# Attention over a cached sequence, one query: the value product with 8 positions x 64 columns per multiplication instead of 2 positions x 192 columns

## The chip, the core and the metric

The kernel runs on one core of a Trainium2 chip. The core has a matrix engine (TensorE; PE in the profile, with PEld for its weight loads), a vector engine (VectorE, DVE), an activation engine (ScalarE, ACT), a general engine (GpSimd, POOL) and a synchronising engine (SyncE, SP). Here SP issues nearly all transfers from HBM into the on-chip memory; 16 DMA engines carry them out. PE writes its sums into a separate accumulation memory (PSUM), from which DVE and ACT read.

The metric is the device time of one execution in microseconds (us), the median of several runs. The profile comes from one more execution, which has a time of its own.

## The reference

One token goes through a transformer block whose normalisations are modulated by a condition `c`. Nearly all of the data is the cache: 32 heads of 8192 positions of 192 numbers, once for keys and once for values, 32-bit, 201 MB each. Cut to its core:

```python
mod = (silu(c) @ w_mod).reshape(1, 6, 1, 640)
sa, ca, ga, sb, cb, gb = (mod[:, k] for k in range(6))

h = layernorm(x) * (1 + ca) + sa
q = (h @ wq).reshape(1, 1, 32, 192).transpose(0, 2, 1, 3)
scores = einsum("bhqd,bhkd->bhqk", q, k_cache) * 192 ** -0.5
o = einsum("bhqk,bhkd->bhqd", softmax(scores), v_cache)
x = x + ga * (o.transpose(0, 2, 1, 3).reshape(1, 1, 6144) @ wo)

h = layernorm(x) * (1 + cb) + sb
x = x + gb * (relu(h @ w1 + b1) ** 2 @ w2 + b2)
```

## The kernel before

**Layout.** A head's 8192 positions lie on the 128 partitions, 64 consecutive positions on each, so a head's keys are one tile of 128 x 12288 numbers (6.3 MB), and its values another. Three such slots (`slot`, L48) hold keys, values and, at the start and the end, the dense weights. `load` (L149) issues one transfer for a tile; the last heads' tiles are cut in two or four (`CUTS`, L32). All of these transfers are issued by SP in the order of the program: k, the pair's weights, v, head after head. A transfer into a slot waits until the work that read the slot's last tile is done: a k transfer waits for the value multiplications of an earlier head, a v transfer for the key sums of an earlier head.

**Keys** (`keys`, L182). With one query there is no matrix product worth PE's while: in four chunks of 16 positions DVE multiplies the tile by the query, which stands on all partitions (L189), POOL folds six of the sixteen products in half (L192), DVE sums nine (L193) and the six folded ones (L194), and ACT sums one (L197). Between the chunks come pieces of other heads' work, in an order written out by hand (`between`, L272): in even heads `project` of the pair before after chunk 1 and `attend` after chunk 2, in odd heads the next pair's `query` after chunk 2. After chunk 0 comes `inverse` of the head before.

**Softmax** (`softmax`, L211). DVE takes the largest score of each partition, PE spreads these over the partitions with the identity, and DVE takes the largest of all. ACT then writes the exponentials, each 16 times (`p`, 128 x 64 x 16, L221), and their sum per partition, which PE adds over the partitions (`total`, L86). `inverse` (L205) takes one over that sum on DVE and multiplies it by a mask of two columns, which chooses between two positions.

**Values** (`values`, L225). For each of 32 pairs of positions, PE takes the pair's 2 x 16 copies of exponentials as stationary operand (32 columns) and the two positions' 384 numbers as the moving one (L232). The pair's number modulo 4 names the strip of 32 columns of the array, and so the 32 partitions of the sum, to which it is added. The first 16 rows of a strip's sum hold what is wanted in columns 0 to 191, the other 16 in columns 192 to 383; the rest is a product of one position's weight with the other's values.

**Output projection** (`project`, L237, and `attend`, L249). For each head of a pair DVE scales the first half of the sum by the mask's first column (L243), and adds the second half times the second column (L244). Three PE multiplications with ones add the rows and turn the 384 results onto partitions (L247), DVE copies them (L251), and 12 multiplications with the rows of `wo` add to the accumulator `att` (L255).

**The end.** After the last head come the last pair's `project` and `attend`, the second normalisation (its sums over partitions are multiplications with ones, L89), the remaining columns of the modulation (`mod`, L128), and the dense part (L317, L320 to L323, L333). Its weights go into slots as these come free: `w1_t` behind the last keys, `gw_t` behind the last values, the latter in three pieces (L294). The last product (L333) needs the second and third pieces for its second half and its last block.

Of the kernel before, what the change touches and what calls it, by code (L numbers as in the profile page):

```python
# [8 lines left out]
F32 = mybir.dt.float32  # L9
AF = mybir.ActivationFunctionType  # L10
ALU = mybir.AluOpType
AX = mybir.AxisListType

P = 128
D = 640
H = 32
SK = 8192
DH = 192
FF = 1536
G = 4  # L20
DG = D // G
FG = FF // G
KB = DG // 32
FB = FG // 32
PW = 2 * DH
NPAIR = H // 2
NPOS = SK // P
I = 16
# [4 lines left out]
WO = 3 * D  # L33
WQ = KB * PW
W2_CUT = ((0, 6), (6, 5), (11, 1))
# [4 lines left out]
def block_kernel(ctx: ExitStack, tc: tile.TileContext, xc, kc, vc, wq0, wx, wo15, wm0, wm1, w1, gw2, bb, out):  # L40
    nc = tc.nc
    const = ctx.enter_context(tc.tile_pool(name="const", bufs=1))
    strm = ctx.enter_context(tc.tile_pool(name="strm", bufs=3))
    work = ctx.enter_context(tc.tile_pool(name="work", bufs=2))
# [3 lines left out]
    def slot(name):  # L48
        return strm.tile([P, NPOS * DH], F32, tag="slot", name=name, bufs=3)


    ident = const.tile([P, P], F32, name="ident")
    make_identity(nc, ident)
    ones = const.tile([P, P], F32, name="ones")
    nc.vector.memset(ones, 1.0)

    mask = const.tile([P, 2], F32, name="mask")
    nc.vector.memset(mask[:, 0:1], 0.0)
    nc.vector.memset(mask[:, 1:2], 1.0)
    for g in range(G):  # L60
        nc.vector.memset(mask[32 * g:32 * g + 16, 0:1], 1.0)
        nc.vector.memset(mask[32 * g:32 * g + 16, 1:2], 0.0)
    eps_t = const.tile([P, 1], F32, name="eps_t")
    nc.vector.memset(eps_t, EPS)

# [6 lines left out]
    def columns(src, n, name, pool=const, **how):  # L72

        t = pool.tile([P, n // 32, 32], F32, name=name, **how)
        nc.vector.transpose(t.rearrange("p b r -> p (b r)"), src)
        return t
# [9 lines left out]
    def total(src, name):  # L86

        ps = psum.tile([P, 512], F32, tag="sm", name="ps_" + name, bufs=2)
        nc.tensor.matmul(ps[:, :1], ones, src, start=True, stop=True)  # L89
        return ps[:, :1]  # L90
# [23 lines left out]
    e = const.tile([P, KB], F32, name="silu")  # L114
# [22 lines left out]
    def load_w(i):  # L137

        w_t[i] = strm.tile([P, WO + WQ], F32, tag="w", name=f"w{i}", bufs=2)
        if i < 0:  # L140
            nc.sync.dma_start(w_t[i][:, WO:], wq0)
        elif i + 1 == NPAIR:
            nc.sync.dma_start(w_t[i][:, :WO], wo15)
# [3 lines left out]
    k_t, v_t = {}, {}  # L147

    def load(src, to, h, what):  # L149
        to[h] = slot(f"{what}{h}")  # L150
        n = CUTS.get((what, h), 1)
        w = NPOS * DH // n
        for c in range(n):
            nc.sync.dma_start(to[h][:, c * w:(c + 1) * w],
                              src[h].rearrange("(p i) d -> p (i d)", p=P)[:, c * w:(c + 1) * w])

    load_w(-1)
    load(kc, k_t, 0, "k")
# [12 lines left out]
    def query(i):  # L171
        w = w_t[i - 1][:, WO:].rearrange("p (b n) -> p b n", b=KB)
        ps = psum.tile([P, 512], F32, tag="q", name=f"ps_q{i}", bufs=2)
        for b in range(KB):
            nc.tensor.matmul(ps[:, :PW], hR[:, b], w[:, b], start=(b == 0), stop=(b == KB - 1))  # L175
        qb_t[i] = work.tile([P, PW], F32, name=f"qb{i}", tag="qb")
        nc.scalar.activation(qb_t[i], ps[:, :PW], AF.Copy, scale=DH ** -0.5)

# [24 lines left out]
    ri_t, ps_t, sum_t = {}, {}, {}  # L203

    def inverse(h):  # L205
        r = work.tile([P, 1], F32, tag="r", name=f"r{h}")
        nc.vector.reciprocal(r, sum_t.pop(h))
        ri_t[h] = work.tile([P, 2], F32, tag="ri", name=f"ri{h}", bufs=3)
        nc.vector.tensor_scalar(ri_t[h], mask, r, None, op0=ALU.mult)

    def softmax(h, sc):  # L211
        mp = work.tile([P, 1], F32, tag="mp", name=f"mp{h}")
        nc.vector.tensor_reduce(mp, sc, axis=AX.X, op=ALU.max)  # L213
        ps = psum.tile([P, 512], F32, tag="sm", name=f"ps_mx{h}", bufs=2)
        nc.tensor.matmul(ps[:, :P], mp.to_broadcast([P, P]), ident, start=True, stop=True)  # L215
        nm = work.tile([P, 1], F32, tag="nm", name=f"nm{h}")
        nc.vector.tensor_reduce(nm, ps[:, :P], axis=AX.X, op=ALU.max, negate=True)  # L217

        p = work.tile([P, NPOS, 16], F32, tag="p", name=f"p{h}", bufs=1)
        sp = work.tile([P, 1], F32, tag="sp", name=f"sp{h}")  # L220
        nc.scalar.activation(p, sc[:, :, None].to_broadcast([P, NPOS, 16]), AF.Exp, bias=nm, accum_out=sp)  # L221
        sum_t[h] = total(sp, f"sum{h}")
        return p

    def values(h, p):  # L225

        t = v_t.pop(h)
        ps_t[h] = psum.tile([P, 512], F32, tag="o", name=f"ps_o{h}", bufs=3)
        n = NPOS // 2
        for j in range(n):  # L230
            g = j % G
            nc.tensor.matmul(ps_t[h][32 * g:32 * (g + 1), :PW], p[:, 2 * j:2 * j + 2].rearrange("p e r -> p (e r)"),  # L232
                             t[:, PW * j:PW * (j + 1)], start=(j < G), stop=(j >= n - G))

    os_t = {}

    def project(i):  # L237

        os_ = work.tile([P, PW], F32, tag="os", name=f"os{i}")
        for a in range(2):  # L240
            h = 2 * i + a
            o, ps, ri = os_[:, DH * a:DH * (a + 1)], ps_t.pop(h), ri_t.pop(h)
            nc.vector.tensor_scalar(o, ps[:, :DH], ri[:, 0:1], None, op0=ALU.mult)  # L243
            nc.vector.scalar_tensor_tensor(o, ps[:, DH:PW], ri[:, 1:2], o, op0=ALU.mult, op1=ALU.add)  # L244
        os_t[i] = psum.tile([P, 512], F32, tag="sm", name=f"ps_oT{i}", bufs=2)
        for j in range(3):
            nc.tensor.matmul(os_t[i][:, 32 * j:32 * (j + 1)], os_[:, P * j:P * (j + 1)], ones[:, :32], start=True, stop=True)  # L247

    def attend(i):  # L249
        oT = work.tile([P, 96], F32, tag="oT", name=f"oT{i}")  # L250
        nc.vector.tensor_copy(oT, os_t.pop(i)[:, :96])  # L251
        w = w_t.pop(i)[:, :WO].rearrange("p (j n) -> p j n", j=3)
        for j in range(3):
            for g in range(G):
                nc.tensor.matmul(att[32 * g:32 * (g + 1), :DG], oT[:, 32 * j:32 * (j + 1)],  # L255
                                 w[:, j, DG * g:DG * (g + 1)],
                                 start=(i == 0 and j == 0), stop=(i == NPAIR - 1 and j == 2))

    x_t = spread(x_c, KB, "x_t")
    bbt = spread(bbc, FB + KB, "bbt")  # L260
    for h in range(H):
        i = h // 2
# [9 lines left out]
        def between(c):  # L272
            if c == 1 and h % 2 == 0 and h:
                project(i - 1)
            elif c == 2 and h % 2 == 0 and h:
                attend(i - 1)
            elif c == 2 and h % 2 and i + 1 < NPAIR:
                query(i + 1)

        sc = keys(h, between)  # L280
        p = softmax(h, sc)
# [9 lines left out]
    a = 0  # L291
    for b0, n in W2_CUT:
        b = KB * D + (b0 + n) * D
        nc.sync.dma_start(gw_t[:, a:b], gw2[:, a:b])  # L294
        a = b
    w1_t = w1_t[:, :KB * FF].rearrange("p (b n) -> p b n", b=KB)
    w2_t = gw_t[:, KB * D:(KB + FB) * D].rearrange("p (b n) -> p b n", b=FB)

    inverse(H - 1)
    project(NPAIR - 1)  # L300
    attend(NPAIR - 1)
    x1 = const.tile([P, DG], F32, name="x1")
# [12 lines left out]
    for b in range(KB):  # L315
        for g in range(G):
            nc.tensor.matmul(pf[32 * g:32 * (g + 1), :FG], hT2[:, b], w1_t[:, b, FG * g:FG * (g + 1)],  # L317
                             start=(b == 0), stop=(b == KB - 1))
    f = work.tile([P, FG], F32, name="f", tag="spread", bufs=1)
    nc.vector.tensor_add(f, pf[:, :FG], bbt[:, :FG])  # L320
    nc.vector.tensor_scalar(f, f, 0.0, None, op0=ALU.max)
    nc.vector.tensor_mul(f, f, f)
    fT = columns(f, FG, "fT", work, tag="os")  # L323

    mod(5, 1, gw_t[:, :KB * D].rearrange("p (b n) -> p b n", b=KB))
    gb2 = const.tile([P, DG], F32, name="gb2")
# [4 lines left out]
    for b in range(FB):  # L331
        for g in range(G):
            nc.tensor.matmul(py[32 * g:32 * (g + 1), :DG], fT[:, b], w2_t[:, b, DG * g:DG * (g + 1)],  # L333
                             start=(b == 0), stop=(b == FB - 1))
# [45 lines left out]
```

## Time and profile before

| | |
|---|---|
| time, median of 3 runs | 1060.53 us (1060.53 to 1060.59) |
| the profiled execution: time | 1060.67 us |
| the profiled execution: span from the first instruction to the last | 1058.8 us |
| read from HBM | 451.82 MB, 427 GB/s over the span |
| busy: DVE, PE, POOL, ACT | 821.6, 417.6, 180.4, 110.1 us |
| mean granted clock of PE | 0.645 of full speed |

In the profile, a row of a group names the line, the engine, the operation, what it writes and reads (out<-in), the shape and the count; then the busy time in us and the mean duration of one in ns; then the idle time of the engine just before them and what ended most of it. A row of the timeline begins with the start and the duration in us, and the bracket at its end is the idle time before it. A row of the chain of waits has a start, a duration and what set the end in that time. PE's 32-bit multiplications leave two records each, and each record has a weight load.

### The profile page before, as it was taken

Reading aid. Unit: us, or ns where it says so; the run is one execution under the profiler, and the core shown is the slowest. Engines: PE = TensorE matmul, PEld = TensorE weight load, DVE = VectorE, ACT = ScalarE, POOL = GpSimd, SP = SyncE. Lnnn points to the kernel's source line nnn. Section 1 sums busy time; section 2 is a strip of 40 time slices with the busy share of each in tenths; the row PEclk is TensorE's granted clock in tenths of the full one; section 3 lists DMA queues with packets and bytes.
Section 4 is the critical chain, followed back from the end, with each engine's and each line's share of the span. In section 5 each row is a group of like instructions: output and inputs, shape, how many; then the busy total and the mean of one; then the engine's idle time right before and its main releaser. Section 6 shows DMA issues by size and latency. Waiting matters only on the chain.

```text
span 1058.8 us, 7905 instructions
## 1 busy us (share of the span) xinstructions
PE 417.6 (39%) x3120; PEld 188.3 (18%) x3120; DVE 821.6 (78%) x646; ACT 110.1 (10%) x343; POOL 180.4 (17%) x134
## 2 busy tenths in 40 slices
PE   3043532435344144533434353143534424353446
PEld 1011211112121111211111121111212111121223
DVE  2986868878686996868788686897868698689952
ACT  1010101101001010110101010110101101011110
POOL 0211212212111221211212111221212121122210
PEclk8566665666656566665666666566665666666667
DMA  9999999999999999999999999999999999999997
GB/s 399 444 428 420 433 441 419 445 427 430 439 435 418 434 437 436 430 425 430 439 427 433 433 430 435 423 436 440 430 430 431 431 432 435 429 431 430 410 433 300
DMA packets 14013, 452.33 MB, mean 427 GB/s; under 512 B 1812, under 2 KB 1816, under 8 KB 2200
## 3 DMA queue, kind: packets, MB, share of 16 engines
q1 hardware_dynamic: 13688, 451.81, 99.2%
q8 instruction: 24, 0.39, 0.2%
q14 instruction: 13, 0.11, 0.0%
q10 hardware_dynamic: 288, 0.01, 0.0%
HBM read 451.82 MB, written 0.00 MB: 427 GB/s over the span
## 4 chain that ended last, share of the span: by engine, by line
DVE 42%; DMA 40%; PE 15%; ACT 2%; issue 1%; POOL 0%; DVEq 0%; SPq 0%; ACTq 0%
DMA k<-in_kc 36%; DVE k L189 21%; DVE sc L193 12%; PE ps_o L232 11%; DVE sc L194 4%; DMA gw_t<-in_gw 2%; ACT p L221 2%; PE ps_mx L215 1%; DVE os L244 1%; DMA xct<-in_xc 1%; DVE os L243 1%; PE ps_sum L89 1%; PE ps_mod L128 1%; PE ps_q L175 1%; DVE nm L217 0%
## 5 line engine op out<-in xcount | busy, mean ns | idle before, releaser
L189 DVE TENSOR_TENSOR k<-k,qb 128x3072 f32<-128x3072 f32 x128 | 429.0, 3352 | 151.2 <-DMA k<-in_kc 146.8
L192 POOL TENSOR_TENSOR k<-k 128x576 f32<-128x576 f32 x128 | 179.7, 1404 | 835.8 <-DVE k L189 821.1
L193 DVE TENSOR_REDUCE sc<-k 128x9 f32<-128x1728 f32 x128 | 250.2, 1954 | 4.4
L232 PE MATMUL ps_o<-v,p 128*32 128x384 f32 x2048 | 238.9, 636 | 0.0
L215 PE MATMUL ps_mx<-ident,mp 128*128 128x128 f32 x64 | 25.4, 501 | 308.5 <-DVE mp L213 308.5
L197 ACT ACTIVATE jk<-k 128x192 f32<-128x192 f32 x128 | 46.5, 363 | 769.2 <-DVE k L189 751.2
L232 PEld LDWEIGHTS ps_o<-v,p 128*32 128x32 f32 x2048 | 75.5, 139 | 141.9 <-issue 141.3
L247 PE MATMUL ps_oT<-ones,os 128*128 128x32 f32 x96 | 26.5, 400 | 175.9 <-DVE os L244 173.7
L194 DVE TENSOR_REDUCE sc<-k 128x6 f32<-128x576 f32 x128 | 95.0, 743 | 0.1
L215 PEld LDWEIGHTS ps_mx<-ident,mp 128*128 128x128 f32 x64 | 16.0, 311 | 327.4 <-DVE mp L213 302.1
L255 PE MATMUL att<-w,oT 128*32 128x160 f32 x384 | 28.4, 463 | 75.6 <-DVE oT L251 75.6
L247 PEld LDWEIGHTS ps_oT<-ones,os 128*128 128x128 f32 x96 | 22.2, 310 | 189.1 <-DVE os L244 188.5
L175 PE MATMUL ps_q<-w,hR 128*128 128x384 f32 x150 | 52.4, 496 | 0.0
L221 ACT ACTIVATE p<-sc,nm 128x1024 f32<-128x1024 f32 x32 | 36.7, 1147 | 114.2 <-DVE nm L217 114.2
L89 PE MATMUL ps_sum<-sp,ones 128*128 128x1 f32 x64 | 18.8, 363 | 56.2 <-ACT p L221 56.2
L175 PEld LDWEIGHTS ps_q<-w,hR 128*128 128x128 f32 x150 | 27.3, 190 | 25.3 <-issue 9.4
L217 DVE TENSOR_REDUCE nm<-ps_mx 128x1 f32<-128x128 f32 x32 | 9.3, 291 | 28.5 <-PE ps_mx L215 28.5
L255 PEld LDWEIGHTS att<-w,oT 128*32 128x32 f32 x384 | 15.5, 161 | 81.9 <-DVE oT L251 77.7
L89 PEld LDWEIGHTS ps_sum<-sp,ones 128*128 128x128 f32 x64 | 16.1, 312 | 65.6 <-ACT p L221 65.6
L197 ACT ACTIVATION_READ_ACCUMULATOR jk<-k 128x1 f32 x128 | 23.9, 187 | 0.0
L128 PE MATMUL ps_mod<-wm_t,silu 128*32 128x320 f32 (+1 forms) x120 | 12.6, 599 | 12.4 <-DVE silu L118 12.4
L243 DVE TENSOR_SCALAR os<-ps_o,ri 128x192 f32<-128x192 f32 x32 | 13.1, 408 | 5.3 <-PE ps_o L232 5.3
(72 smaller groups left out, 105.5 us busy)
## 6 DMA issues: line engine op xcount, KB each, us to landing
v<-in_vc SPq DMA_DIRECT2D x31, 6144.0 KB, 23.9
k<-in_kc SPq DMA_DIRECT2D x30, 6144.0 KB, 26.8
w<-in_wx SPq DMA_DIRECT2D x15, 1920.0 KB, 32.3
wm_t<-in_wm SPq DMA_DIRECT2D x2, 3200.0 KB, 26.9
k<-in_kc SPq DMA_DIRECT2D x2, 3072.0 KB, 21.8
k<-in_kc SPq DMA_DIRECT2D x4, 1536.0 KB, 21.5
v<-in_vc SPq DMA_DIRECT2D x4, 1536.0 KB, 16.3
w_t<-in_w SPq DMA_DIRECT2D x1, 3840.0 KB, 23.2
```

The costliest lines, as they stand in the source:

```text
L89: nc.tensor.matmul(ps[:, :1], ones, src, start=True, stop=True)
L175: nc.tensor.matmul(ps[:, :PW], hR[:, b], w[:, b], start=(b == 0), stop=(b == KB - 1))
L189: nc.vector.tensor_mul(pr, pr, q[:, None, :].to_broadcast([P, I, DH]))
L192: nc.gpsimd.tensor_add(half, half, pr[:, m:n, DH // 2:])
L193: nc.vector.tensor_reduce(sc[:, c * I:c * I + m], pr[:, :m], axis=AX.X, op=ALU.add)
L194: nc.vector.tensor_reduce(sc[:, c * I + m:c * I + n], half, axis=AX.X, op=ALU.add)
L197: nc.scalar.activation(jk, pr[:, i], AF.Copy, accum_out=sc[:, c * I + i:c * I + i + 1])
L215: nc.tensor.matmul(ps[:, :P], mp.to_broadcast([P, P]), ident, start=True, stop=True)
L221: nc.scalar.activation(p, sc[:, :, None].to_broadcast([P, NPOS, 16]), AF.Exp, bias=nm, accum_out=sp)
L232: nc.tensor.matmul(ps_t[h][32 * g:32 * (g + 1), :PW], p[:, 2 * j:2 * j + 2].rearrange("p e r -> p (e r)"), t[:, PW * j:PW * (j + 1)], star ...
L247: nc.tensor.matmul(os_t[i][:, 32 * j:32 * (j + 1)], os_[:, P * j:P * (j + 1)], ones[:, :32], start=True, stop=True)
L255: nc.tensor.matmul(att[32 * g:32 * (g + 1), :DG], oT[:, 32 * j:32 * (j + 1)], w[:, j, DG * g:DG * (g + 1)], start=(i == 0 and j == 0), sto ...
```

## The change

The value product is laid out otherwise. One multiplication now takes eight positions, four copies of each exponential (again 32 stationary columns), and of each of the eight positions the same 64 of the 192 columns (512 moving columns). A head needs 8 groups of positions times 3 groups of columns (`NV`), 24 multiplications; the column group names the strip, so strips 0 to 2 are used and strip 3 is not. The values are put into this order before the launch. In a strip's sum, row r belongs to position r // 4, and of its 8 blocks of 64 columns only the block of that position is wanted: `project` multiplies the sum by one over the total and by a mask of eight columns in one instruction, and a second one adds the eight blocks. The head's result then stands as 64 columns on 96 partitions, and one multiplication with `quad` (ones in three diagonal blocks of 32 x 32) adds the rows of each strip and turns both heads' results onto partitions. The rows of `wo` are put into the matching order. `inverse` is left with the reciprocal. `kc` is handed over in another shape with the same bytes.

```diff
+E = 8
+ED = 64
+NV = DH // ED
...
-    mask = const.tile([P, 2], F32, name="mask")
-    nc.vector.memset(mask[:, 0:1], 0.0)
-    nc.vector.memset(mask[:, 1:2], 1.0)
-    for g in range(G):
-        nc.vector.memset(mask[32 * g:32 * g + 16, 0:1], 1.0)
-        nc.vector.memset(mask[32 * g:32 * g + 16, 1:2], 0.0)
+    mask = const.tile([P, E], F32, name="mask")
+    nc.vector.tensor_reduce(mask, ident.rearrange("p (g e c) -> p e g c", g=G, e=E), axis=AX.XY, op=ALU.add)
+    quad = const.tile([P, 32 * NV], F32, name="quad")
+    nc.vector.memset(quad, 0.0)
+    for g in range(NV):
+        nc.vector.memset(quad[32 * g:32 * (g + 1), 32 * g:32 * (g + 1)], 1.0)
...
     def inverse(h):
-        r = work.tile([P, 1], F32, tag="r", name=f"r{h}")
-        nc.vector.reciprocal(r, sum_t.pop(h))
-        ri_t[h] = work.tile([P, 2], F32, tag="ri", name=f"ri{h}", bufs=3)
-        nc.vector.tensor_scalar(ri_t[h], mask, r, None, op0=ALU.mult)
+        ri_t[h] = work.tile([P, 1], F32, tag="ri", name=f"ri{h}", bufs=3)
+        nc.vector.reciprocal(ri_t[h], sum_t.pop(h))
...
-        p = work.tile([P, NPOS, 16], F32, tag="p", name=f"p{h}", bufs=1)
+        p = work.tile([P, NPOS, 32 // E], F32, tag="p", name=f"p{h}", bufs=1)
         sp = work.tile([P, 1], F32, tag="sp", name=f"sp{h}")
-        nc.scalar.activation(p, sc[:, :, None].to_broadcast([P, NPOS, 16]), AF.Exp, bias=nm, accum_out=sp)
+        nc.scalar.activation(p, sc[:, :, None].to_broadcast([P, NPOS, 32 // E]), AF.Exp, bias=nm, accum_out=sp)
...
     def values(h, p):
 
-        t = v_t.pop(h)
+        t = v_t.pop(h).rearrange("p (j g n) -> p j g n", g=NV, n=E * ED)
         ps_t[h] = psum.tile([P, 512], F32, tag="o", name=f"ps_o{h}", bufs=3)
-        n = NPOS // 2
+        n = NPOS // E
         for j in range(n):
-            g = j % G
-            nc.tensor.matmul(ps_t[h][32 * g:32 * (g + 1), :PW], p[:, 2 * j:2 * j + 2].rearrange("p e r -> p (e r)"),
-                             t[:, PW * j:PW * (j + 1)], start=(j < G), stop=(j >= n - G))
+            for g in range(NV):
+                nc.tensor.matmul(ps_t[h][32 * g:32 * (g + 1)], p[:, E * j:E * (j + 1)].rearrange("p e r -> p (e r)"),
+                                 t[:, j, g], start=(j == 0), stop=(j == n - 1))
...
     def project(i):
 
-        os_ = work.tile([P, PW], F32, tag="os", name=f"os{i}")
+        n = 32 * NV
+        os_ = work.tile([P, 2, ED], F32, tag="os", name=f"os{i}")
         for a in range(2):
             h = 2 * i + a
-            o, ps, ri = os_[:, DH * a:DH * (a + 1)], ps_t.pop(h), ri_t.pop(h)
-            nc.vector.tensor_scalar(o, ps[:, :DH], ri[:, 0:1], None, op0=ALU.mult)
-            nc.vector.scalar_tensor_tensor(o, ps[:, DH:PW], ri[:, 1:2], o, op0=ALU.mult, op1=ALU.add)
+            om = work.tile([P, E, ED], F32, tag="om", name=f"om{h}", bufs=1)
+            nc.vector.scalar_tensor_tensor(om[:n], ps_t.pop(h)[:n].rearrange("p (e d) -> p e d", e=E), ri_t.pop(h)[:n],
+                                           mask[:n, :, None].to_broadcast([n, E, ED]), op0=ALU.mult, op1=ALU.mult)
+            nc.vector.tensor_reduce(os_[:n, a], om[:n].rearrange("p e d -> p d e"), axis=AX.X, op=ALU.add)
         os_t[i] = psum.tile([P, 512], F32, tag="sm", name=f"ps_oT{i}", bufs=2)
-        for j in range(3):
-            nc.tensor.matmul(os_t[i][:, 32 * j:32 * (j + 1)], os_[:, P * j:P * (j + 1)], ones[:, :32], start=True, stop=True)
+        nc.tensor.matmul(os_t[i][:, :n], os_[:n].rearrange("p a d -> p (a d)"), quad[:n], start=True, stop=True)
...
-    fT = columns(f, FG, "fT", work, tag="os")
+    fT = columns(f, FG, "fT", work, tag="om", bufs=1)
...
-    wo = a(A_wo).reshape(NPAIR, 3, P, D).transpose(0, 2, 1, 3).reshape(NPAIR, P, WO)
+    wo = a(A_wo).reshape(NPAIR, 2, NV, ED, D).transpose(0, 1, 3, 2, 4).reshape(NPAIR, P, WO)
...
-        "kc": np.ascontiguousarray(a(A_k_cache).reshape(H, SK, DH)),
-        "vc": np.ascontiguousarray(a(A_v_cache).reshape(H, SK, DH)),
+        "kc": np.ascontiguousarray(a(A_k_cache).reshape(H, P, NPOS * DH)),
+        "vc": a(A_v_cache).reshape(H, P, NPOS // E, E, NV, ED).transpose(0, 1, 2, 4, 3, 5).reshape(H, P, NPOS * DH),
```

More of the change, by code (lines that the diff above doesn't have):

```diff
@@ L154, in load @@
             nc.sync.dma_start(to[h][:, c * w:(c + 1) * w],
-                              src[h].rearrange("(p i) d -> p (i d)", p=P)[:, c * w:(c + 1) * w])
+                              src[h][:, c * w:(c + 1) * w])
     load_w(-1)
```

## The prediction

> **What bounds the kernel now.** I read the page's busy shares and DMA rows first, then the stretches, the transfers, and at last the chain of waits at the end.
>
> ```profile
> span 1058.8 us, 7905 instructions
> PE 417.6 (39%) x3120; PEld 188.3 (18%) x3120; DVE 821.6 (78%) x646; ACT 110.1 (10%) x343; POOL 180.4 (17%) x134
> ...
> DMA  9999999999999999999999999999999999999997
> ```
>
> The 16 DMA engines are full in 39 of 40 slices; no engine is. Next the stretches (busy time and count for PE, PEld, DVE, ACT, POOL, then granted clock, DMA share, GB/s):
>
> ```profile
> 400.00:600.00 200.00, 83.17 (x593) 35.88 (x593) 155.49 (x113) 20.02 (x65) 34.10 (x25) 0.64 1.00 431
> ...
> 1027.20:1034.05 6.85, 5.73 (x78) 2.71 (x70) 1.13 (x4) 0.00 (x0) 0.00 (x0) 1.00 1.01 431
> 1034.05:1040.88 6.83, 4.72 (x32) 2.36 (x36) 1.90 (x8) 0.26 (x1) 0.00 (x0) 0.50 1.04 447
> ...
> 1044.29:1047.70 3.41, 3.41 (x28) 1.26 (x24) 0.00 (x0) 0.00 (x0) 0.00 (x0) 0.50 0.94 400
> 1047.70:1057.80 10.10, 6.63 (x156) 4.58 (x148) 3.65 (x9) 0.00 (x0) 0.00 (x0) 1.00 0.35 142
> ```
>
> The rate is 431 GB/s with DVE 78% busy and 431 with DVE nearly idle: what the engines do does not set it, and the change moves the same tensor bytes. Only a starved queue could lose time in the loop. How far is it from that?
>
> ```profile
> v<-in_vc SPq DMA_DIRECT2D x31, 6144.0 KB, 23.9
> k<-in_kc SPq DMA_DIRECT2D x30, 6144.0 KB, 26.8
> ...
> SPq L154 <- PE ps_o L232: 326.3, 31, 11.7
> ```
>
> 6144 KB (6.29 MB) at 431 GB/s take 14.6 us, but a k transfer lands 26.8 us after its issue and a v transfer 23.9 us: 12.2 and 9.3 us of earlier bytes lie ahead of each. The k issue is the one that waits for the value multiplications (third row); PE may be some 12 us later per head, and DVE some 9 us, before a DMA engine idles.
>
> So the change shows at the end alone. The chain there (start, us, what):
>
> ```profile
> 948.18 18.39 DMA k<-in_kc
> 966.66 3.37 DVE k L189
> ...
> 972.77 0.23 DVE ri L209
> ...
> 978.91 0.34 DVE os L243
> ...
> 980.46 3.28 DVE k L189
> ...
> 999.98 0.23 DVE ri L209
> ...
> 1019.53 1.25 ACT p L221 x2
> ...
> 1024.23 6.76 PE ps_o L232 x64
> ...
> 1031.39 21.96 DMA gw_t<-in_gw
> 1053.39 1.88 PE ps_y L333 x48
> ```
>
> From the landing of the first half of k30 (966.6) DVE never waits for a transfer again; keys 30 and 31, softmax, values 31 and the dense block follow one another. The last weights land at 1053.35, and the second half of the last multiplications waits for them:
>
> ```profile
> PEld ps_y L333 <- DMA gw_t<-in_gw: 0.4, 1, 0.4
> ```
>
> So two chains end almost together: the transfers, and the computation with 0.4 us to spare. Later computation costs what exceeds that; earlier computation gains nothing, since what follows 1053.39 stays.
>
> **The change, part by part.**
>
> *Value multiplications.* 24 of 512 columns replace 32 of 384, both 12,288 columns per head; but 24 use three column strips of the array, 32 used four.
>
> ```profile
> L232 PE MATMUL ps_o<-v,p 128*32 128x384 f32 x2048 | 238.9, 636 | 0.0
> ...
> 22.13 5.95 PE L175 MATMUL ps_q<-w-1_101,hR 128*128 128x384 f32 x10 [1.94 <-DVE hR L169]
> ...
> 1025.29 0.19 PEld L232 LDWEIGHTS ps_o<-v,p 128*32 128x32 f32 x4 [0.45 <-issue]
> 1025.93 0.19 PEld L232 LDWEIGHTS ps_o<-v,p 128*32 128x32 f32 x4 [0.45 <-issue]
> ...
> 1029.80 0.12 PEld L232 LDWEIGHTS ps_o<-v,p 128*32 128x32 f32 x4 [0.20 <-issue]
> 1030.12 0.12 PEld L232 LDWEIGHTS ps_o<-v,p 128*32 128x32 f32 x4 [0.20 <-issue]
> ...
> 1031.02 0.42 DVE L243 TENSOR_SCALAR os<-ps_o,ri 128x192 f32<-128x192 f32 x1 [5.29 <-PE ps_o L232]
> ```
>
> 2048 records for 1024 multiplications: two each, on one strip, one behind the other. Four records go as a turn, 0.64 us after the one before until the clock steps to full at 1027.20, and 0.32 us after it from then on. A turn is therefore two multiplications on two strips, not one on each of four. Full-width records of the same length take 0.60 us each (5.95/10), about what a whole slow turn takes, so a turn moves four streams at once. Weights load one turn ahead: the load at 1030.12 belongs to the last turn, which starts about 1030.45 and is read at 1031.02, 0.57 us later. Were two passes still to be run behind one another on the later strips (0.64 us), the reader could not start there. With two strips busy at a time, the third suffices: 24 x 512 columns are 12 turns of 0.32 x 512/384 = 0.43 us, 5.1 us at full clock, as 16 x 0.32 now. One cost is new: the next turn now returns to a strip that is still in use, so its weights may load late, 0.11 to 0.19 us once (the loads' own length), after which the turns are staggered and hide it. Bounds: nothing, or, if a turn never goes past the third strip, 16 turns of 0.43 us, +1.7 us. I take +0.1, the row of two strips being the nearest.
>
> *DVE turns per pair.* Two instructions per head become a 512-element product and a 512-element sum.
>
> ```profile
> L193 DVE TENSOR_REDUCE sc<-k 128x9 f32<-128x1728 f32 x128 | 250.2, 1954 | 4.4
> L194 DVE TENSOR_REDUCE sc<-k 128x6 f32<-128x576 f32 x128 | 95.0, 743 | 0.1
> L244 DVE SCALAR_TENSOR_TENSOR os<-ps_o,ri,os 128x192 f32<-128x192 f32 x32 | 13.4, 418 | 1.1
> ```
>
> Slope (1954 - 743)/1152 = 1.05 ns an element. Sum: 743 - 64 x 1.05 = 0.68 us; product: 418 + 320 x 1.05 = 0.75 us. The sum steps 64 elements between addends, which no row shows: between the price of contiguous elements and double, +0.68 us each; I take the former. In keys 30 the turn of pair 14 now lasts 980.46 - 978.91 = 1.55 us; then 2 x 1.43 = 2.88 us with its handovers (the one `om` buffer makes the second product wait for the first sum): **+1.33**. What is queued behind it on DVE is the next key product, and behind that every later key chunk. In earlier pairs DVE's waits for k hide this, 9 us deep.
>
> *The mask product of `inverse`* goes: twice on this chain, 2 x 0.23: **-0.46** (the third lies under values 31).
>
> *Exponential of 4 copies instead of 16.*
>
> ```profile
> L221 ACT ACTIVATE p<-sc,nm 128x1024 f32<-128x1024 f32 x32 | 36.7, 1147 | 114.2 <-DVE nm L217 114.2
> L197 ACT ACTIVATE jk<-k 128x192 f32<-128x192 f32 x128 | 46.5, 363 | 769.2 <-DVE k L189 751.2
> ```
>
> (1147 - 363)/832 = 0.94 ns an element, 768 fewer: **-0.72**. Bounds: with no fixed share 1.12 ns, -0.86; with L193's slope -0.81; nothing if it were all fixed, which 363 at 192 excludes.
>
> *Last pair.* Head 30's part lies under values 31; head 31's does not.
>
> ```profile
> 1031.47 0.42 DVE L244 SCALAR_TENSOR_TENSOR os<-ps_o,ri,os 128x192 f32<-128x192 f32 x1
> 1031.95 0.63 PE L247 MATMUL ps_oT<-ones,os 128*128 128x32 f32 x4 [0.67 <-DVE os L244]
> 1032.62 0.26 DVE L251 COPY oT<-ps_oT 128x96 f32<-128x96 f32 x1 [0.72 <-PE ps_oT L247]
> 1032.93 1.02 PE L255 MATMUL att<-w,oT 128*32 128x160 f32 x24 [0.35 <-DVE oT L251]
> ```
>
> 0.87 us (1031.02 to 1031.89) becomes 0.75 + 0.68 + 0.03 = 1.46; one multiplication of 96 columns costs about what the four short records do, +0.05: **+0.64**.
>
> *Instruction loading.* 512 + 64 multiplication records and as many loads fall out: 1152 of the 7905 instructions, 15%.
>
> ```profile
> q8 instruction: 24, 0.39, 0.2%
> ```
>
> An estimate: 15% of 0.39 MB is 0.14 us at 431 GB/s, 15% of that queue's share of the span (0.2%, 2.1 us) 0.3 us. Both chains start from transfers, so both come **0.2** earlier.
>
> ```profile
> 11.76 0.17 DVE L116 TENSOR_SCALAR silu<-silu 128x5 f32<-128x5 f32 x1 [10.20 <-ACT silu L115]
> ```
>
> The new constants (`mask`, `quad`) are made in these 10.2 us of waiting; loads cover the same rows of bytes, and wo's new order is made before the launch: nothing.
>
> *Sum.* 1.33 - 0.46 - 0.72 + 0.1 + 0.64 = +0.89; less the spare 0.4: +0.49. The clock rows shift this: the dense multiplications stand in half-speed stretches that end at fixed times (1040.88, 1047.70), and work pushed beyond those ends runs at double speed; against that L255 is pushed towards the half speed from 1034.05. I take -0.2 for both, -0.2 for instructions: +0.1. The profiled execution took 1060.67 (1.9 outside its span); the median of the runs shown is 0.14 lower: 1060.53 + 0.1, rounded up for the untried stride: **1060.7**.
>
> **Rivals.**
>
> *The transfers alone decide.* If product and sum cost less, or the clock returns more, the spare covers all: 1060.53 - 0.2 = 1060.3. For it: backlog and rate. Against: only 0.4 us of spare.
>
> *Three strips take three quarters of the rate* (the slower side). Place: values 31. Price +1.7 as bounded; 0.89 - 0.1 + 1.7 = 2.5, L255 then runs at half speed, +0.8 (most of its 1.02 us again), less 0.4 and 0.2: +2.7, 1063.2. It decides from about +1.4 us in values 31. Against: two strips per turn. It has 15%.
> The Trainium skill bears on this: TensorE: Matmul & The Clock Gate, section Measured speedup vs the span model, gives 2.38x for three column tiles and 3.07x for four row tiles. An estimate by that page: values 3.07/2.38 = 1.29 times as long, some +2 us where this trace's turns of two give none.
>
> *The strided sum costs double.* Three sums on the chain, +2.0: 1062.7. No row speaks for or against; the gate is whether `project`'s sums measure 0.7 or 1.4 us.
>
> *The change doesn't do what it says:* fewer multiplications, same columns, so PE's busy time does not fall. This is part of the forecast. A real gain would need the last landing to come early; only instruction bytes can do that.
>
> **How the numbers follow.** Forecast 52%, transfers alone 20%, three strips 15%, stride 8%, unnamed 5%. A measurement can tell about 0.2% (2.1 us) from no change: same is 1058.4 to 1062.6. Slower: most of the three strips, half of the stride and of the unnamed, 18%. Faster: half of the unnamed, 3%. Same: 79%. The range runs from 1060.1 (transfers alone with the larger saving) to 1063.2 (three strips). The likeliest case alone: 1060.2 to 1061.3.
>
> **What would show it.** Values: 1536 records, busy near 240 us in all, four loads per turn of 0.43 us; with three strips serial, 300 us or more. DMA full in 39 slices; the k issue still about 12 us ahead. Sums near 0.7 us and products near 0.75. The exponential near 0.42 us. PE's wait for `gw_t` shrinks from 0.4 to none. I am wrong if the loop's rate leaves 431 GB/s, if the last weights land elsewhere than 1053, or if DVE's wait for k disappears.

## The result, and the profile after

The changed kernel took 1062.64 us (median of 15 runs, 1061.46 to 1063.51), the kernel before beside it 1060.57 (15 runs, 1060.41 to 1062.60). The ratio is 1.0018, with a 95% interval from 1.0011 to 1.0025: slower by 0.18%, a little less than the 0.2% that the prediction took as its bound, with an interval that reaches past it. The profiled execution took 1063.15 us.

From the page of the changed kernel: the span, the busy shares, the DMA row, the instruction queue, and four groups (the new line numbers are one to three higher).

```profile
span 1061.4 us, 6745 instructions
...
PE 459.8 (43%) x2544; PEld 168.9 (16%) x2544; DVE 845.1 (80%) x609; ACT 89.7 (8%) x343; POOL 180.4 (17%) x134
...
DMA  9999999999999999999999999999999999999996
...
q8 instruction: 20, 0.33, 0.1%
...
L233 PE MATMUL ps_o<-v,p 128*32 128x512 f32 x1536 | 295.7, 743 | 0.0
...
L247 DVE TENSOR_REDUCE os<-om 96x64 f32<-96x512 f32 x32 | 32.3, 1008 | 1.1
...
L245 DVE SCALAR_TENSOR_TENSOR om<-ps_o,ri,mask 96x512 f32<-96x512 f32 x32 | 23.7, 741 | 7.8 <-PE ps_o L233 6.2
...
L222 ACT ACTIVATE p<-sc,nm 128x256 f32<-128x256 f32 x32 | 16.2, 508 | 114.2 <-DVE nm L218 114.2
```

The DMA engines are as full as before, so the loop is still theirs. But PE's value records are busy 295.7 us instead of 238.9, although the columns streamed are the same, and the strided sum takes 1.01 us. The new product takes 0.74 us, as expected; the exponential takes 0.51, where 0.42 was expected. Two rows of its transfers (the last column is us from issue to landing) and then SP's wait for the value multiplications (total, count, longest) show that the longer values are hidden in the loop:

```profile
v<-in_vc SPq DMA_DIRECT2D x31, 6144.0 KB, 24.2
k<-in_kc SPq DMA_DIRECT2D x30, 6144.0 KB, 26.3
```

```profile
SPq L157 <- PE ps_o L233: 361.2, 31, 13.1
```

SP waits 361 us for values instead of 326, but a k transfer still lands 26.3 us after its issue, 11.7 us more than its bytes need (26.8 and 12.2 before). The delay took half a microsecond of a cover of twelve.

The chain at the end (start, us, what), in the same order as the rows of before:

```profile
965.88 3.37 DVE k L192
...
971.88 0.07 DVE ri L210
...
977.86 0.67 DVE om L245
978.55 1.02 DVE os L247
...
981.45 3.28 DVE k L192
...
1020.26 0.61 ACT p L222 x2
...
1024.32 8.39 PE ps_o L233 x48
1032.73 0.76 DVE om L245
...
1035.39 1.07 PE att L257 x24
...
1054.38 3.50 PE ps_y L335 x96
1057.90 0.34 DVE y L338
```

Two rows of the kernel before are needed beside these, the last product in its timeline, and the last step of its chain:

```profile
1051.46 3.77 PE L333 MATMUL ps_y<-gw_t,fT 128*32 128x160 f32 x96 [0.23 <-DVE fT L75]
```

```profile
1055.30 0.34 DVE y L336
```

The transfer of the last weights has left the chain: the last product runs through in one piece from 1054.38. Each difference of two starts is now a term, and the terms add up to the 2.6 us between the spans:

| stretch of the chain | before, us | after, us | difference | predicted |
|---|---|---|---|---|
| landing of k30, up to the first key product | 966.66 | 965.88 | -0.78 | -0.2 |
| the pair's turn on DVE in keys 30 | 1.55 | 3.59 | +2.04 | +1.33 |
| the rest of keys 30 and 31 (two masks of `inverse` gone) | 51.32 | 50.79 | -0.53 | -0.46 |
| exponential to the start of values 31 | 4.70 | 4.06 | -0.64 | -0.72 |
| values 31, up to the reader | 6.79 | 8.41 | +1.62 | +0.1 |
| last turn of the pair, up to `att` | 1.91 | 2.66 | +0.75 | +0.64 |
| `att` to the last product (clock) | 18.53 | 18.99 | +0.46 | -0.2 |
| last product (its wait for weights gone) | 3.84 | 3.52 | -0.32 | -0.4 |

The pair's turn is 981.45 - 977.86 after and 980.46 - 978.91 before; the others are differences of starts of the quoted rows. Three terms that add time are far off: values 31, the turns with the strided sum, and the clock. A second profiled execution of the changed kernel took 1063.70 us and started the first key product of keys 30 at 966.22, so the first row, -0.78 here, is -0.44 there.

The last of the three is seen in the stretches of the clock behind values 31 (PEclk is the column behind POOL's):

```profile
1027.18:1037.42 10.24, 6.97 (x65) 2.26 (x59) 2.89 (x6) 0.00 (x0) 0.00 (x0) 1.00 1.02 437
1037.42:1044.24 6.82, 5.71 (x40) 2.78 (x44) 1.05 (x6) 0.26 (x1) 0.00 (x0) 0.50 0.97 417
1044.24:1047.66 3.42, 1.32 (x20) 0.47 (x16) 1.79 (x5) 0.00 (x0) 0.00 (x0) 1.00 0.96 409
1047.66:1051.07 3.41, 3.41 (x28) 1.39 (x23) 0.00 (x0) 0.00 (x0) 0.00 (x0) 0.50 0.96 401
```

Full speed begins where it did before (1027.2), but lasts 10.24 us instead of 6.83, and all later steps come 3.4 us later than before.

How PE deals the records out is seen in the weight loads of values 31 (timeline of the changed kernel; the bracket is the idle time ahead):

```profile
1024.95 0.19 PEld L233 LDWEIGHTS ps_o<-v,p 128*32 128x32 f32 x3 [0.66 <-issue]
1025.80 0.19 PEld L233 LDWEIGHTS ps_o<-v,p 128*32 128x32 f32 x3 [0.66 <-issue]
...
1031.21 0.12 PEld L233 LDWEIGHTS ps_o<-v,p 128*32 128x32 f32 x3 [0.31 <-issue]
1031.64 0.12 PEld L233 LDWEIGHTS ps_o<-v,p 128*32 128x32 f32 x3 [0.31 <-issue]
```

Three records to a turn, no longer four; 0.85 us from turn to turn at half clock, 0.43 at full. 48 records are 16 turns, where the prediction had counted 12.

### The profile page after: what moved, and what is told of

Read it like the earlier page. It is cut to its first block, busy times and chain, and to the rows that moved or that the text cites. A ratio compares the mean times of both kernels' runs of the same rounds, so it can differ in the third digit from the quotient of the medians.

```text
span 1061.4 us, 6745 instructions
## 1 busy us (share of the span) xinstructions
PE 459.8 (43%) x2544; PEld 168.9 (16%) x2544; DVE 845.1 (80%) x609; ACT 89.7 (8%) x343; POOL 180.4 (17%) x134
## 4 chain that ended last, share of the span: by engine, by line
DVE 45%; DMA 33%; PE 19%; issue 2%; ACT 1%; POOL 0%; DVEq 0%; ACTq 0%
DMA k<-in_kc 32%; DVE k L192 21%; PE ps_o L233 14%; DVE sc L196 12%; DVE sc L197 4%; DVE os L247 3%; DVE om L245 2%; PE ps_mx L216 1%; PE ps_mod L131 1%; DMA xct<-in_xc 1%; PE ps_sum L92 1%; PE ps_q L178 1%; PE ps_f L319 0%; ACT p L222 0%; DVE nm L218 0%
## 5 line engine op out<-in xcount | busy, mean ns | idle before, releaser
L233 PE MATMUL ps_o<-v,p 128*32 128x512 f32 x1536 | 295.7, 743 | 0.0
L233 PEld LDWEIGHTS ps_o<-v,p 128*32 128x32 f32 x1536 | 69.5, 133 | 197.9 <-issue 197.3
L249 PE MATMUL ps_oT<-quad,os 96*128 96x96 f32 x32 | 11.6, 464 | 201.1 <-DVE os L247 201.1
L249 PEld LDWEIGHTS ps_oT<-quad,os 96*128 96x128 f32 x32 | 7.8, 303 | 215.6 <-DVE os L247 215.6
L247 DVE TENSOR_REDUCE os<-om 96x64 f32<-96x512 f32 x32 | 32.3, 1008 | 1.1
L245 DVE SCALAR_TENSOR_TENSOR om<-ps_o,ri,mask 96x512 f32<-96x512 f32 x32 | 23.7, 741 | 7.8 <-PE ps_o L233 6.2
L222 ACT ACTIVATE p<-sc,nm 128x256 f32<-128x256 f32 x32 | 16.2, 508 | 114.2 <-DVE nm L218 114.2
## 6 DMA issues: line engine op xcount, KB each, us to landing
k<-in_kc SPq DMA_DIRECT2D x30, 6144.0 KB, 26.3
```

The source lines that it names most:

```text
L233: nc.tensor.matmul(ps_t[h][32 * g:32 * (g + 1)], p[:, E * j:E * (j + 1)].rearrange("p e r -> p (e r)"), t[:, j, g], start=(j == 0), stop=( ...
L245: nc.vector.scalar_tensor_tensor(om[:n], ps_t.pop(h)[:n].rearrange("p (e d) -> p e d", e=E), ri_t.pop(h)[:n], mask[:n, :, None].to_broadca ...
L247: nc.vector.tensor_reduce(os_[:n, a], om[:n].rearrange("p e d -> p d e"), axis=AX.X, op=ALU.add)
```

## The experiments

All were timed beside the kernel before, whose medians were 1060.73, 1060.63, 1060.61 and 1060.60 us in the four groups. The single times spread over 1.4 to 2.6 us in most kernels, so a median of 11 runs is good to some tenths; what follows rests on rows first and on times second.

### Strips: four in the changed kernel, three in the kernel before

```diff
 # changed kernel, values()
+                m = NV * j + g
+                s = m % G
-                nc.tensor.matmul(ps_t[h][32 * g:32 * (g + 1)], ..., t[:, j, g], start=(j == 0), stop=(j == n - 1))
+                nc.tensor.matmul(ps_t[h][32 * s:32 * (s + 1)], ..., t[:, j, g], start=(m < G), stop=(m >= NV * n - G))
```

> The changed kernel with its 24 value multiplications of a head dealt over all four strips in turn (multiplication 3j+g on strip (3j+g) mod 4) instead of three. The sums of a strip then mix the three column groups; what they are used for is left as it is, so the output is not the reference's. Only the strip of each multiplication changes. Theory A, a strip takes its own records one after another and all used strips run side by side, so three strips give three quarters of the rate: turns of 4 records again, 12 of 0.43 us at full clock instead of 16; values 31 last about 6.9 us instead of 8.6, all heads' value records are busy about 240 us instead of 296, and the time falls by about 1.6 us, from 1062.6 to about 1061.0. Theory B, it is the 512 columns or the return of weights to a strip in use, not the number of strips: values stay near 9.2 us a head, 1062.6.

The reader takes three strips as before, so DVE's work is that of the changed kernel; one multiplication in four goes to a strip that is not read. Two loads of values 31 in the timeline, and the group of all value records:

```profile
1029.22 0.12 PEld L235 LDWEIGHTS ps_o<-v,p 128*32 128x32 f32 x4 [0.31 <-issue]
1029.65 0.12 PEld L235 LDWEIGHTS ps_o<-v,p 128*32 128x32 f32 x4 [0.31 <-issue]
```

```profile
L235 PE MATMUL ps_o<-v,p 128*32 128x512 f32 x1536 | 239.4, 789 | 0.0
```

Four records to a turn of the same 0.43 us, and 239.4 us in all, as before the change. 512 columns cost nothing by themselves, and the length of a turn does not depend on how many strips take part. The time was 1061.40 (1060.15 to 1062.76; ratio to the kernel before 1.0003, 0.9994 to 1.0012), 1.2 us under the changed kernel, where 1.6 was expected; the two were not timed in one group.

```diff
 # kernel before
-            g = j % G
+            g = j % 3
-                             ..., start=(j < G), stop=(j >= n - G))
+                             ..., start=(j < 3), stop=(j >= n - 3))
-            o, ps, ri = os_[:, ...], ps_t.pop(h), ri_t.pop(h)
+            o, ps, ri = os_[:96, ...], ps_t.pop(h)[:96], ri_t.pop(h)[:96]
-            nc.tensor.matmul(..., os_[:, P * j:P * (j + 1)], ones[:, :32], ...)
+            nc.tensor.matmul(..., os_[:96, P * j:P * (j + 1)], ones[:96, :32], ...)
```

> The kernel before with one edit: its 32 value multiplications of 384 columns go over three strips (j mod 3) instead of four, and what reads the sums reads 96 partitions. Theory A: 22 turns of 0.32 us at full clock instead of 16, +1.9 us in values 31; the chain at the end has 0.4 us to spare, so the time rises by about 1.5, to 1062.1, and it varies from run to run as the changed kernel's does. Theory B: no change, 1060.6.

The same two views of this kernel:

```profile
1028.98 0.12 PEld L232 LDWEIGHTS ps_o<-v,p 128*32 128x32 f32 x3 [0.21 <-issue]
1029.30 0.12 PEld L232 LDWEIGHTS ps_o<-v,p 128*32 128x32 f32 x3 [0.21 <-issue]
```

```profile
L232 PE MATMUL ps_o<-v,p 128*32 128x384 f32 x2048 | 299.7, 597 | 0.0
```

The mirror image: the old multiplication on three strips takes three records every 0.32 us, and 299.7 us instead of 238.9. The time rose less than expected, to 1061.07 (1060.55 to 1062.17), 0.3 us over its partner, and the ratio (1.0000, 0.9991 to 1.0009) does not tell it from the kernel before. The profiled execution is the longest (1062.17), and its last product runs in one piece, so there the computation is the later chain; of the short ones there is no trace. The rows show the mechanism; what it costs in time differs from run to run, and this experiment does not settle it.

### The stride of the sum

```diff
-            om = work.tile([P, E, ED], F32, ...)
+            om = work.tile([P, ED, E], F32, ...)
-                ... ps.rearrange("p (e d) -> p e d", e=E), ri, mask[:n, :, None].to_broadcast([n, E, ED]) ...
-            nc.vector.tensor_reduce(os_[:n, a], om[:n].rearrange("p e d -> p d e"), axis=AX.X, op=ALU.add)
+                ... ps.rearrange("p (d e) -> p d e", e=E), ri, mask[:n, None, :].to_broadcast([n, ED, E]) ...
+            nc.vector.tensor_reduce(os_[:n, a], om[:n], axis=AX.X, op=ALU.add)
 # values: column, then position, within the 512 columns
```

> The changed kernel with the 512 columns of a multiplication in the order column-position instead of position-column (values laid out so before the launch), so that the sum over the eight blocks reads eight neighbouring elements instead of eight that lie 64 apart. Theory A, the stride makes the sum 1.01 us instead of 0.68: it falls to about 0.7 us, the product stays at 0.74, three sums on the chain, so the time falls by about 1.0 us, to 1061.6. Theory B, the 64 short groups of eight cost it, whatever their stride: the sum stays at 1.0 us, 1062.6.

The group of its sums:

```profile
L247 DVE TENSOR_REDUCE os<-om 96x64 f32<-96x512 f32 x32 | 21.8, 682 | 1.1
```

1008 ns become 682, for the same 512 elements and 64 results; 0.68 is the price the prediction had taken. The product, whose order changes with it, stays at 0.74. So it is the stride, 64 elements of 4 bytes, and not the short groups. The time was 1060.94 (1060.66 to 1062.24; ratio to the kernel before 1.0003, 0.9994 to 1.0011), 1.7 us under the changed kernel, which was timed in another group, where the three sums on the chain explain 1.0. The rest is not explained by a row, and lies within the spread of either; the profiled executions, 1062.07 and 1063.15, differ by 1.1.

### The clock at the end

```diff
+WARM = {2: 5, 3: 3}
 # keys(), after between(c)
+            if h == H - 1 and c in WARM:
+                idle = psum.tile([P, 512], F32, tag="q", ...)
+                for _ in range(WARM[c]):
+                    nc.tensor.matmul(idle, ones, <512 elements of this chunk's products>, start=True, stop=True)
```

> The changed kernel with eight more multiplications (ones times 512 elements of the last keys' products) on PE in the last head, five after its third chunk and three after its fourth, where PE was idle; their sums are read by nobody. Theory A, the end is set by PE running at half clock after its idle time: the modulation's 40 records last 1.5 us instead of 2.9, values 31 about 7.1 instead of 8.6, the chain of computation ends about 2.9 us earlier, the last weights set the end again: 1060.3 to 1060.7, and the spread over the runs (2.05 us in the changed kernel) shrinks to a few tenths. Theory B, the last weights, which land at 1053.9 instead of 1053.3, and not PE set the end: no more than 0.2 us are gained, 1062.5.

Two rows of its chain, and two stretches:

```profile
1021.44 1.50 PE ps_mod L132 x40
1022.93 6.89 PE ps_o L238 x48
```

```profile
1015.01:1032.00 16.99, 14.01 (x105) 5.90 (x104) 8.13 (x11) 2.34 (x5) 1.41 (x1) 1.00 1.02 437
1032.07:1042.31 10.24, 7.77 (x65) 3.76 (x68) 2.19 (x9) 0.26 (x1) 0.00 (x0) 0.50 1.02 438
```

Where PE had been busy, it ran at full clock: the modulation took 1.50 us instead of 2.82, values 31 6.89 instead of 8.39. But in the gaps behind them the clock fell again (0.50 from 1032.07), and the next modulation took 5.2 us at half speed. The time fell to 1060.90 (1060.19 to 1062.03; ratio to the kernel before 0.9994, 0.9985 to 1.0003); the spread, 1.84 us, hardly shrank, against the expectation. The next pair of kernels filled those gaps too:

```diff
 # kernel before; and the changed kernel with the contiguous sum
+    spare = psum.tile([P, 512], F32, tag="o", ...)
+    def spin(n):
+        for _ in range(n):
+            nc.tensor.matmul(spare[:, :P], ones, ones, start=True, stop=True)
+    # 3 behind the last values, 4 behind attend, 4 behind the mean, 7 behind the second modulation;
+    # WARM = {2: 4, 3: 2}
```

> The kernel before with extra multiplications that nobody reads, put where PE would be idle in the last head and behind it (six of 512 columns in the last keys, then 3, 4, 4 and 7 of 128 columns in the gaps of the last projection, the normalisation and ahead of the dense part), so that the clock stays at full speed. Theory A, the end is the later of two chains, the last weights and a computation whose length hangs on the clock: modulation 2.8 us instead of 4.7, the dense product 3.3 instead of 5.1, values 31 5.2 instead of 6.9, the chain of computation some 5 us earlier, and what is left is the landing of the last weights: 1059.8, at most 0.4 us between the runs. Theory B, the spread and the end come from the transfers: 1060.6 and single runs up to 1062.8 as in the kernel before.

> The changed kernel with the contiguous sum and the same extra multiplications in the same places. Theory A, all that the change adds lies in the computation behind the last key tiles, and the last weights are where they were: with the clock at full speed this is hidden again, 1059.8 to 1060.0, as the kernel before with these multiplications. Theory B, the change also costs the transfers something in the loop: half a microsecond or more above it.

Both expectations failed: 1061.50 (1060.68 to 1062.48; ratio 1.0006, 0.9998 to 1.0015) from the kernel before and 1061.37 (1060.57 to 1062.65; 1.0007, 0.9998 to 1.0016) from the changed one. No gain came, and the medians are 0.9 and 0.7 us above the kernel before, though the intervals reach 1. Two stretches of the first, with a row of its chain, show where the gain went:

```profile
1044.90:1049.45 4.55, 0.00 (x0) 0.00 (x0) 2.05 (x4) 0.00 (x0) 0.00 (x0) 1.00 0.93 388
1049.47:1052.88 3.41, 3.09 (x48) 2.72 (x52) 0.14 (x1) 0.00 (x0) 0.00 (x0) 0.50 0.60 247
```

```profile
1049.79 2.90 PE ps_mod L131 x40
```

The computation did come four microseconds earlier: the dense product was done at 1044.9, in the kernel before at 1049.1. Then PE stood still until the first piece of the last weights landed, the clock fell to half for the next 3.41 us, and the last modulation took 2.90 us instead of 1.56. The early computation lost its clock while it waited. 18 more multiplications fill that wait:

```diff
 # behind the dense product
+    spin(18)
```

> The kernel before with the extra multiplications of the last experiment and 18 more of 128 columns behind the dense product, where PE waited 4.9 us for the last weights and the clock fell to half. Theory A, clock and last weights together set the end: the last modulation lasts 1.5 us instead of 2.9, the last product is done within 0.3 us of the third piece's landing at about 1054.2, 1059.9, and the runs lie within half a microsecond, without single ones at 1062. Theory B, the extra multiplications themselves cost time (they stand in PE's queue ahead of the real ones): 1061 or more as in the last experiment.

One of PE's waits for the last weights, and two stretches:

```profile
PE ps_y L350 <- DMA gw_t<-in_gw: 0.5, 1, 0.5
```

```profile
1026.75:1044.70 17.95, 17.18 (x198) 9.94 (x190) 4.81 (x16) 0.26 (x1) 0.00 (x0) 1.00 0.99 422
...
1049.70:1057.40 7.70, 5.03 (x136) 4.36 (x136) 1.63 (x5) 0.00 (x0) 0.00 (x0) 1.00 0.23 94
```

The clock is full from 1026.75 to the end, and the transfer of the last weights sets the end. The time is 1060.65 (ratio 0.9996, 0.9987 to 1.0005), no gain, but all runs lie between 1060.48 and 1060.83, while 5 of the 20 runs of the kernel before beside it are above 1061.4. The expected 1059.9 had let the last product end 0.3 us behind the third piece; its second half, six blocks, takes 1.88 us and starts only when the second piece has landed, at 1053.47 here. This is the floor that the transfers set in this layout. With the clock held no run rises above it, so the long runs of the kernel before are put down to a computation that was late by the clock; this is argued, since no long run of it was profiled.

> The changed kernel with the contiguous sum and the same extra multiplications, those 18 among them. Theory A: 1059.9 as its partner from the kernel before, within 0.2 us, since behind a computation that is early by some microseconds all that the change adds is hidden; its runs lie close together. Theory B, the change costs the transfers or the loop something: half a microsecond or more above its partner.

1060.44 (1059.75 to 1061.63; ratio to the kernel before 0.9995, 0.9986 to 1.0004), 0.2 us under its partner. With the clock held, the three strips (the sum is the contiguous one here) cost nothing that can be told from zero, as theory A had it, though its runs do not lie close together.

### The two terms together, and the changed kernel again

> The changed kernel as it is, beside the others on the same chip. 1061.5 to 1063.5, median about 1062.5; both theories.

1062.65 (1061.41 to 1063.70; ratio 1.0014, 1.0004 to 1.0023), the same as at first.

The next one has both edits, the four strips and the contiguous sum:

> The changed kernel with the contiguous sum and with the value multiplications dealt over four strips (the sums then mix the column groups and the output is not the reference's). It takes both terms away that were sized too small. Theory A, these two are the difference from the forecast: values 31 about 6.9 us, sums 0.68, the end 1060.6, within 0.2 us of the kernel before beside it, with single runs up to 1062.8 as there. Theory B, something else in the change costs time: 1061.5 or more.

1060.63 (1059.83 to 1061.20), the kernel before beside it 1060.63 (ratio 0.9998, 0.9989 to 1.0007), the changed kernel 1062.65. Two rows of its chain:

```profile
1023.87 6.70 PE ps_o L235 x48
...
1051.29 3.50 PE ps_y L337 x96
```

Values 31 last 6.70 us, and the last product starts at 1051.29, as in the kernel before (1051.46). The two edits together give back the 2.0 us, and no other part of the change need be blamed. Their single gains, 1.2 and 1.7 us, do not add up to more, which fits a floor that the transfers set.

### Less of the last product behind the last weights

```diff
-W2_CUT = ((0, 6), (6, 5), (11, 1))
+W2_CUT = ((0, 6), (6, 3), (9, 2), (11, 1))
```

> The changed kernel with the contiguous sum and all the extra multiplications, and the last weights in four pieces (6, 3, 2 and 1 blocks) instead of three (6, 5, 1), so that less of the last product waits for a late piece. Theory A, the landing of the last weights sets the end: three blocks (0.8 us of the last product) move ahead of the landing at about 1053, the product ends about 0.6 us earlier, 1059.8 beside 1060.4. Theory B, a further piece only moves the landing: 1060.4.

> The kernel before with all the extra multiplications and the same four pieces. Theory A: 1060.0 to 1060.1 beside 1060.65, all runs within half a microsecond. Theory B: 1060.6. What remains between this and its partner from the changed kernel, 0.2 us in the experiment before, is then the difference in instruction bytes.

1060.15 (1059.40 to 1061.52) from the changed kernel, 1060.32 (1060.13 to 1060.93) from the kernel before; the kernel before as it is 1060.60 beside them. The ratios are 0.9996 (0.9987 to 1.0004) and 0.9997 (0.9988 to 1.0006), so neither is told from 1 by its interval; of the latter's 11 runs, 7 lie under the lowest of the 21 runs beside it (1060.49). If it is a gain, it is half of the expected one, some 0.3 us.

## Why the prediction was right in its range and wrong in its likeliest case

- *The transfers bound the loop, and the change shows at the end alone:* held. DMA stays full, 431 GB/s, the cover of a k transfer shrinks from 12.2 to 11.7 us, and once both terms at the end are taken back (1060.63 against 1060.63), or the sum's taken back and the clock held (1060.44 against 1060.65), no difference is seen.
- *The value multiplications, +0.1:* this step failed: "A turn is therefore two multiplications on two strips, not one on each of four." A turn has as many records as there are strips in use: three in the changed kernel and in the kernel before on three strips, four in both on four. One record of each strip fits this, though the trace names no strip. The bound of the other side, 16 turns and +1.7, is what happened (+1.62). The inference had taken the order of issue for the order of work. The two records of a multiplication are issued one behind the other on one strip, yet four start within a turn; it followed only if they start in that order. The check by the reader, 0.57 us after the last turn, excludes work behind that turn; it says nothing of which records are in it. The right count is the strip's own: 24 multiplications on three strips are 8 on each, 16 records of 512 columns; 32 on four are also 8 on each, 16 records of 384.
- The estimate by the Trainium skill, TensorE: Matmul & The Clock Gate, section Measured speedup vs the span model, was 3.07/2.38 = 1.29 between its four row tiles and its three column tiles. The traces give 295.7/238.9 = 1.24 over all heads with the clock's changes, 1.33 by turns at one clock: they agree with that estimate far better than with the forecast.
- *The turns on DVE:* the product was priced well (0.75 against 0.74), the sum at the lower of its two bounds, 0.68 against 1.01. The Trainium skill, SBUF — State Buffer, section Door 1: The DMA port swizzle, says that accesses in one line of 16 bytes run at full rate and each new line costs; that section gives no size. The 256-byte steps here take 1008/512 = 1.97 ns an element, neighbours 682/512 = 1.33, which is the way of that rule. With two of the three sums in it and a handover of 0.1 us between the first sum and the second product, the term of the pair's turn was 2.04 instead of 1.33. The last turn holds the third sum, yet came at 0.75 against 0.64, since the one multiplication with `quad` brought the way from `os` to `att` down from 0.98 us to 0.82.
- *Exponential and `inverse`:* -0.64 and -0.53 against -0.72 and -0.46. The 768 elements of the exponential went for 0.64 us (1147 - 508 ns), 0.83 ns each, not the 0.94 that the slope between two kinds of instruction had given.
- *The spare of 0.4 us* was used up as said, -0.32 here.
- *The clock steps, -0.2:* wrong in sign in this execution (+0.46). The step that failed is "half-speed stretches that end at fixed times (1040.88, 1047.70)": they ended at 1044.24 and 1051.07, 3.4 us later, behind a full-speed stretch that lasted 3.4 us longer. So the second modulation ran wholly at half speed, 5.1 us instead of 4.7, which is this term, and the product with `wo`, which was to be pushed towards half speed, ran at full (1.02 us, as before). Where the steps lie also differs from run to run. They are not the whole of the changed kernel's spread, 2.05 us: its two profiled executions differ by 0.55 us, of which 0.34 lie ahead of keys 30, and with the clock held its runs still spread over 1.9. The rest of the cause is open.
- *Instruction bytes, -0.2:* 0.06 MB less were loaded (0.33 instead of 0.39). In the nine profiles of the new layout, all with 0.33 MB, keys 30 start between 965.88 and 966.31, in the five of the old one, with 0.39 or 0.41 MB, between 966.23 and 966.67, some 0.4 us later in the mean. That is the way of the forecast, but no run changed the instruction bytes alone, so the link is not shown.

Of the rivals, the three strips came, and of the strided sum's doubled price about half came with them. That the rival's 1063.2 meets the 1063.15 of the profiled execution is luck: its 0.8 us for the product with `wo` at half speed did not come, while 0.7 us of the pair's turn and 0.7 of the clock, which it did not hold, did, and the earlier landing took 0.6 back. The measured 1062.64 lies in the range only because the range reached as far as this rival, which had 15%; the likeliest case had the value multiplications wrong in their mechanism, and that was its largest miss.

## What to carry to other kernels

When the loop is bound by transfers, look for the place where the last transfer's chain and the last computation's chain meet, and price every edit there: here 0.4 us of spare stood against a 12 us cover elsewhere. Count the strips of the array that a layout uses, not its multiplications or its columns: records on one strip follow each other, so the longest strip sets the time. Let a sum read neighbours, where the layout can be chosen before the launch.

## What the runs showed of the hardware that was not expected

- As many records start together as strips are in use, and a turn takes the same time with three as with four: 3 x 512 or 4 x 512 columns in 0.43 us, 3 x 384 or 4 x 384 in 0.32 us. That each strip takes one record per turn, whatever the order of issue, is inferred from this; how records overtake each other is not seen in the trace, which names no strip.
- A sum over elements 64 apart takes 1008 ns, over neighbours 682, for the same 512 elements: 0.64 ns more for each.
- The clock's stretches shown here last 3.41, 6.8 and 10.24 us, multiples of 3.41, but they lie at other places in other executions: in two executions of the changed kernel full speed began at 1027.2 and at 1027.7, in the kernel before on three strips at 1026.5, with the contiguous sum at 1025.9, and with multiplications added ahead of it at 1015.0. The Trainium skill, TensorE: Matmul & The Clock Gate, section Part 1: The HAM clock gate, has a window of 3413 ns that runs free of the kernel's start; the stretches above agree. In one trace a wait of 4.55 us was followed by half clock for 3.41 us.
- The second piece of the last weights landed between 1053.35 and 1053.66 us in four profiles of kernels with the old layout and three pieces, and between 1052.46 and 1053.91 in eight with the new one. This may be why the runs of the changed kernel with the clock held still spread over 1.9 us, against 0.35; its cause was not tried and stays open.
